# FFT convolution before two gated MLPs on one core: first batch's result kept on chip, exchange laid out slots-innermost, start of the MLP reordered

## The chip, the cores and the metric

The kernel runs on one core of one Trainium2 chip, as one launch. The time is device microseconds for the whole launch. Before the change the median of three runs was 1239.99 us (1238.87 to 1240.51).

## The reference

Two batches of 3008 tokens with 256 channels are convolved along the sequence with a filter given in the frequency domain; the 6016 tokens then pass through a gated MLP (SiLU, hidden width 1536) and a second MLP (a clipped gate, hidden width 2048), all in float32.

```python
X = np.fft.rfft(x, axis=1)                              # x: (2, 3008, 256)
y = np.fft.irfft(X * (filt_r + 1j * filt_i), n=3008, axis=1)
x = y.reshape(6016, 256)
g = x @ w_gate                                          # (256, 1536)
x = (g / (1 + np.exp(-g)) * (x @ w_val)) @ w_out        # w_out: (1536, 256)
h = x @ w_in                                            # (256, 2048)
return (h * np.clip(h + 3, 0, 6) / 6) @ w_out2          # (2048, 256)
```

## The kernel before, in words

**The convolution.** 3008 = 47 x 64, and the transform is split into 64-point and 47-point transforms, each a matrix multiplication on TensorE. For batch 0 there are three steps.

1. `time_to_slots` takes a *unit* of x (128 x 512, `x0_unit(u)`, 12 units), multiplies it by `mat[:, 0]` (float32, two passes), has ScalarE copy the result from PSUM into a staging tile (`stage_tile`, six places in the tags `wq`, `sm`, `y`, `g`) and SyncE (SP) store it to the DRAM tensor `d1[0]`. The 64-point transform gives 32 *slots* (frequencies modulo 64), each with 4 rows (real and imaginary, two halves of the other index).
2. `chunk_view` reads `d1` back the other way round: a *chunk* is one or two slots (17 chunks, `CHUNKS`), with 96 partitions that hold the 4 rows x 24 of the other index. In the loop at L484 a chunk gets a 47-point transform (L488), the filter product on VectorE (`filter_product`, L191 to L194, with the final add on GpSimd, or on VectorE for the last two chunks), the inverse 47-point transform two chunks later (L510), a copy by ScalarE (L200) and a store to `d2[0]` (L201, `store_chunk`). Chunks and filters are loaded six ahead (`load_chunk`, `load_filter`). A filter needs `prepare_filter` first (a ScalarE copy, L179, and a product with a sign, L184 on GpSimd or L182 on ScalarE).
3. `load_near` brings the first 8 time columns back with 128 partitions of slots (`near`, three pieces of 64, 48 and 16 partitions), `to_time` (L216) makes two blocks of 512 tokens out of them, and `split_time` splits them into two fp32r parts (ScalarE L148, VectorE L141): `xsd[0]`, `xsd[1]`. The later blocks read `d2[0]` with `load_g`.

**Batch 1** has its units transformed by the same `time_to_slots` (`staged(u)`, L476): four of them right after the chunk loop, eight in the first step of the MLP loop (`p == 0`, L664 to L666). Its chunks are convolved much later, inside the MLP loop (`conv_...`).

**The MLP.** A loop over `t` (two per *step* `p`) does the first MLP: `gate` and `val` for 128 hidden columns, 12 fp32r matmuls of 512 columns, then SiLU (ScalarE, L656), a product (VectorE, L671), a split of the hidden tile (`plain`: ScalarE L148, VectorE L141), and 12 matmuls of the output layer of the step before. The first 12 steps alternate between `xsd[0]` and `xsd[1]`.

**The weights** arrive as 64-bit floats. `Decode` loads them as pairs of words; `start` (ScalarE, L239) takes an absolute value; `word` is six VectorE instructions (L248 to L255 and an add, which is on GpSimd unless an engine is named); `parts_gv` and `parts_o1` split the result into two fp32r parts for the gate and value columns (512 words) and the output columns (256 words) of one group of 128 hidden units. Groups 0 and 1 are loaded during the chunk loop; `lead` (the 512 words) is decoded at `i == n_chunk`, ahead of the last two chunks' copies, `rest` (the 256) after `xsd[1]`. Groups 2, 3, ... follow in the MLP loop, one per step.

**What sets the order.** The schedule is manual: each engine runs its instructions in the order in which the code issues them. All loads and stores go through SP's queue, except six of the first x units, which ScalarE's queue issues (L413). A store that waits for an engine holds up every DMA behind it. Tiles of one tag share a place, so a new one waits for the old one's readers.

Of the kernel before, what the change touches and what calls it, by code (L numbers as in the profile page):

```python
# [16 lines left out]
P = 128  # L17
# [33 lines left out]
def _matrices():  # L51

    n2 = np.arange(N2)
    s1 = np.zeros((2, N2, NS, 2, 2))
    for h in range(2):
        for s in range(NS):
            if s == 0:
                col = np.ones(N2) if h == 0 else (-1.0) ** n2
            elif h == 0:
                col = np.cos(2 * np.pi * (n2 * s % N2) / N2)  # L60
            else:
                col = -np.sin(2 * np.pi * (n2 * s % N2) / N2)
            for c in range(2):
                s1[c, :, s, c, h] = col
# [23 lines left out]
    t = np.zeros((NS, 2, 2, 2, N2))  # L88
    for s in range(NS):
        for c in range(2):  # L90
            if s == 0:
                t[s, c, 0, c] = 1.0 / S
                t[s, c, 1, c] = (-1.0) ** n2 / S
            else:
                a = 2 * np.pi * (n2 * s % N2) / N2
                t[s, c, 0, c] = 2 * np.cos(a) / S
                t[s, c, 1, c] = -2 * np.sin(a) / S

    m2, m20 = (m.reshape(2, 2, H1, 128).transpose(1, 0, 2, 3) for m in (m2, m20))
    i2, i20 = (m.reshape(128, 2, 2, H1).transpose(0, 2, 1, 3) for m in (i2, i20))  # L100
# [8 lines left out]
def fft_conv_glu_mlp(ctx: ExitStack, tc: tile.TileContext, x, filt, mats, sgn, w1, w2, out):  # L109
# [22 lines left out]
    d1 = [dram.tile([P, H1, D], F32, name=f"d1_{b}") for b in range(B)]  # L132
    d2 = [dram.tile([P, H1, D], F32, name=f"d2_{b}") for b in range(B)]
# [23 lines left out]
    def time_to_slots(b, u, src, stage, tag, pieces=1):  # L157
# [4 lines left out]
        for r in range(pieces):  # L162
            part = slice(r * P // pieces, (r + 1) * P // pieces)
            nc.sync.dma_start(out=d1[b][part, 2 * u:2 * u + 2], in_=stage[part].rearrange("p (m c) -> p m c", c=D))
# [5 lines left out]
    def chunk_view(d, i):  # L170

        s0, n = CHUNKS[i]
        return d.rearrange("(s q h) m c -> (q h m) s c", q=2, h=2)[:, s0:s0 + n]
# [24 lines left out]
    def store_chunk(b, i, acc, q):  # L198
        n = CHUNKS[i][1]
        nc.scalar.copy(out=q[:96, :n].rearrange("p s c -> p (s c)"), in_=acc[:96, :n * D])  # L200
        nc.sync.dma_start(out=chunk_view(d2[b], i), in_=q[:96, :n, :])  # L201

    def load_g(b, j, pool=work):
        g = pool.tile([P, 4, D], F32, tag="g", name="g", bufs=1)
        nc.sync.dma_start(out=g, in_=d2[b][:, 4 * j:4 * j + 4])
        return g
# [51 lines left out]
    def decode_w1(f):  # L258
        return Decode(None, w1[:, f, :], 768, w1_place(f))
# [4 lines left out]
    def parts_o1(d, f, engine):  # L264
        o = [wo1[:, f // 2, h, 0:4:3, :] if f % 2 == 0 else wo1[:, f // 2, h, 1:3, :] for h in range(2)]
        split(o[0], o[1], d.w[:, 512:].rearrange("p (a c) -> p a c", c=P), engine)
# [130 lines left out]
    with tc.manual_schedule():  # L397
# [6 lines left out]
        more0 = early.tile([P, 8192], F32, name="more0")  # L404
        raws = mlp.tile([P, 3584], U32, tag="hs", name="raws", bufs=1)
# [6 lines left out]
        for u in range(12):  # L412
            (nc.scalar if u % 2 else nc.sync).dma_start(out=x0_unit(u), in_=x[0, :, u * 512:(u + 1) * 512])  # L413
# [5 lines left out]
        spare = []  # L419

        def stage_tile():

            if not spare:
                y, g = new_y(), work.tile([P, 1024], F32, tag="g", name="g", bufs=1)
                spare.extend([work.tile([P, 512], F32, tag="wq", name="wq", bufs=1),
                              work.tile([P, 512], F32, tag="sm", name="sm", bufs=1),
                              y[:, :512], y[:, 512:], g[:, :512], g[:, 512:]])
# [4 lines left out]
        def load_chunk(i):  # L432
            s0, n = CHUNKS[i]
            bts[i] = more0[:96, i % 6 * 512:][:, :n * D]
            nc.sync.dma_start(out=bts[i].rearrange("p (s c) -> p s c", c=D), in_=chunk_view(d1[0], i))

        def load_filter(i):
            s0, n = CHUNKS[i]
            fts[i] = x0[:, i % 6 * 1024:][:, :n * 2 * D].rearrange("p (s r c) -> p s r c", r=2, c=D)
            nc.sync.dma_start(out=fts[i][0:N1P], in_=filt[0:N1P, s0:s0 + n])  # L440

        for u in range(12):
            time_to_slots(0, u, x0_unit(u), stage_tile(), "gv" if u % 2 else "a", 4 if u == 11 else 1)
            if u == 7:
                load_filter(0)
        for u in range(6):
            nc.tensor.matmul(bank("gv"), mat[:, 0, :], x0_unit(10 + u % 2))
        for i in range(6):
            load_chunk(i)
            if i:  # L450
# [6 lines left out]
        def w1_place(f):  # L457

            if f < 2:
                raw = raws[:, f * 1536:(f + 1) * 1536]  # L460
                a = more0[:, 3072 + f * 1536:][:, :1536]
            else:
                raw = x0[:, f % 2 * 3072:][:, :1536].bitcast(U32)
                a = x0[:, f % 2 * 3072 + 1536:][:, :1536]
            return raw.rearrange("p (n t) -> p n t", t=2), a[:, :768], a[:, 768:]

        units = list(range(12))

        def x1_unit(u):
            k = u + 12 if u < 4 else u - 4 if u < 10 else u + 2  # L470
            return more0[:, k * 512:(k + 1) * 512]
# [4 lines left out]
        def staged(u):  # L476
            time_to_slots(1, u, x1_unit(u), stage_tile(), "a")
# [5 lines left out]
        lead = slice(0, 512)  # L483
        for i in range(n_chunk + 2):  # L484
            if i < n_chunk:
                acc = bank()
                v = bts.pop(i)
                nc.tensor.matmul(acc[:, :v.shape[1]], mat[:96, 1 + alone(i), :], v)  # L488
# [4 lines left out]
                if i + 6 < n_chunk:  # L493
                    load_chunk(i + 6)
                    load_filter(i + 6)
                if i in (6, 9):
                    dec[len(dec)] = decode_w1(len(dec))
                if i > n_chunk - 5:
                    load_x1(i - (n_chunk - 4))
# [7 lines left out]
            if q >= 0:  # L507
                y = ys.pop(q)
                acc = bank("a")
                nc.tensor.matmul(acc[:96, :y.shape[1]], mat[:, 3 + alone(q), :96], y)  # L510
# [23 lines left out]
        left = units[4:]  # L534
        gt = {}
        dec[2].start()
# [4 lines left out]
        def conv_load(c):  # L541
            if 0 <= c < n_chunk:
                s0, n = CHUNKS[c]
                bt = pool.tile([96, 2, D], F32, tag="bt", name="bt", bufs=2)
                nc.sync.dma_start(out=bt[:, :n, :], in_=chunk_view(d1[1], c))
# [57 lines left out]
        for t in range(2 * n_pair):  # L603
# [60 lines left out]
            if p == 0:  # L664
                for u in left[4 * i:4 * (i + 1)]:
                    staged(u)  # L666
# [25 lines left out]
            if t == 0:  # L692
                dec[3].start()

# [187 lines left out]
```

## Time and profile before

| what | value |
|---|---|
| median of three runs | 1239.99 us (1238.87 to 1240.51) |
| profiled execution, its own time | 1241.09 us |
| its span | 1239.3 us |
| mean granted TensorE clock | 0.987 of full |
| busy: TensorE / VectorE / ScalarE / GpSimd | 97% / 86% / 52% / 16% |
| DMA traffic | 86.08 MB, 69 GB/s over the span |

The 1.8 us between span and time lie outside the program. The busy shares are means over stages with very different limits: the convolution of batch 0 and the start of the MLP fill the first 130 us, and of those alone the change touches the program (the layout of `d1` and `d2` also reaches batch 1's convolution from 199 us on).

### The profile page before, as it was taken

How to read it: one execution, taken by the hardware profiler on the slowest of the kernel's cores; microseconds unless marked ns; L12 is line 12 of the kernel's file. 1: busy time of each engine (PE TensorE's matmuls, PEld its weight loads, DVE VectorE, ACT ScalarE, POOL GpSimd, SP SyncE). 2: the span in 40 equal slices, each digit the busy share in tenths (PEclk: the TensorE clock that was granted, in tenths of full speed). 3: DMA queues.
4: the chain of work that ended last, by engine and by line, in shares of the span. 5: the costliest groups of instructions: out<-in, count | busy, mean ns of one | idle time of the engine just before them, and what ended most of it. 6: DMA issues, size and time to landing. Idle time of an engine off the chain costs nothing.

```text
span 1239.3 us, 17614 instructions
## 1 busy us (share of the span) xinstructions
PE 1197.2 (97%) x6722; PEld 1023.6 (83%) x6722; DVE 1068.7 (86%) x1628; ACT 639.4 (52%) x987; POOL 194.8 (16%) x154
## 2 busy tenths in 40 slices
PE   7869999899999999999999999999999999999997
PEld 3236788788889988888888989999989999899997
DVE  1757766999996888877888899999999999999998
ACT  3635445455554444434444555555655565565554
POOL 1704451431110222201222320000000000000000
PEclk9889999899999999999999999999999999999999
DMA  9975313233312222121120320110011001001000
GB/s 278 256 244 176 102 55 99 65 94 94 94 47 78 82 79 76 44 79 49 52 68 1 110 76 1 35 35 15 21 33 35 19 15 35 34 1 35 33 18 16
DMA packets 45428, 86.08 MB, mean 69 GB/s; under 512 B 4784, under 2 KB 23088, under 8 KB 45216
## 3 DMA queue, kind: packets, MB, share of 16 engines
q1 hardware_dynamic: 44480, 83.39, 22.0%
q10 hardware_dynamic: 864, 1.57, 0.4%
q8 instruction: 53, 0.87, 0.3%
q14 instruction: 31, 0.25, 0.1%
HBM read 56.37 MB, written 28.57 MB: 69 GB/s over the span
## 4 chain that ended last, share of the span: by engine, by line
PE 50%; DVE 43%; issue 3%; DMA 2%; POOL 1%; ACT 1%; SPq 0%; DVEq 0%; ACTq 0%; POOLq 0%
PE gv L153 30%; DVE hs L141 14%; PE a L299 12%; DVE h L821 9%; DVE h L141 8%; DVE h L144 3%; PE a L153 2%; PE gv L216 1%; DVE y L371 1%; DVE y L141 1%; DVE xs L141 1%; PE a L160 1%; DMA x<-filt_in 1%; PE a L510 1%; DVE bs L141 1%
## 5 line engine op out<-in xcount | busy, mean ns | idle before, releaser
L299 PEld LDWEIGHTS a<-hs,wall 128*128 128x128 f32 x3276 | 409.0, 189 | 14.0 <-ACT hs L348 1.1
L153 PE MATMUL gv<-xs,wall 128*128 128x512 f32 (+1 forms) x1728 | 412.6, 392 | 7.9 <-DVE u L194 4.4
L299 PE MATMUL a<-hs,wall 128*128 128x256 f32 (+1 forms) x3276 | 416.7, 282 | 2.2 <-ACT hs L348 0.9
L141 DVE TENSOR_TENSOR hs<-h,hs 128x768 fp32r<-128x768 f32 (+2 forms) x324 | 361.9, 1117 | 30.0 <-ACT hs L148 16.6
L153 PEld LDWEIGHTS gv<-xs,wall 128*128 128x128 f32 x1728 | 321.0, 189 | 75.2 <-DVE u L194 5.6
L153 PE MATMUL gv<-xs,wi 128*128 128x512 f32 (+1 forms) x1152 | 275.9, 388 | 0.0
L341 ACT CAST hs<-h 128x768 fp32r<-128x768 f32 (+1 forms) x156 | 128.2, 821 | 261.6 <-DVE h L821 159.7
L153 PEld LDWEIGHTS gv<-xs,wi 128*128 128x128 f32 x1152 | 210.0, 188 | 37.0 <-DVE xs L141 0.4
L348 ACT CAST hs<-h 128x1024 fp32r<-128x1024 f32 (+1 forms) x156 | 160.7, 1030 | 67.4 <-DVE h L141 67.4
L141 DVE TENSOR_TENSOR h<-h 128x512 f32<-128x512 f32 (+3 forms) x312 | 182.4, 585 | 8.7
L671 DVE TENSOR_TENSOR h<-h,gv 128x512 f32<-128x512 f32 (+1 forms) x144 | 96.4, 670 | 40.7 <-PE gv L153 38.4
L821 DVE SCALAR_TENSOR_TENSOR h<-h,gv 128x512 f32<-128x512 f32 (+1 forms) x192 | 128.5, 669 | 0.0
L656 ACT ACTIVATE h<-gv 128x512 f32<-128x512 f32 (+1 forms) x144 | 84.5, 587 | 62.9 <-PE gv L153 62.4
L817 ACT ACTIVATE h<-gv 128x512 f32<-128x512 f32 (+1 forms) x192 | 111.8, 582 | 0.9 <-PE gv L153 0.9
L144 DVE TENSOR_TENSOR h<-h 128x256 f32<-128x256 f32 (+1 forms) x156 | 68.1, 436 | 5.4
L144 POOL TENSOR_TENSOR ww<-ww,wa 128x512 f32<-128x512 f32 x16 | 20.7, 1295 | 216.3 <-DVE wa L255 216.3
L144 POOL TENSOR_TENSOR u<-u,t 128x512 f32<-128x512 f32 (+1 forms) x17 | 20.8, 1225 | 146.0 <-DVE u L194 90.9
L153 PE MATMUL a<-hs,wall 128*128 128x512 f32 x144 | 35.8, 397 | 3.2 <-DVE hs L141 3.2
L191 DVE SCALAR_TENSOR_TENSOR us<-gv,x 64x512 f32<-64x512 f32 (+1 forms) x17 | 11.2, 662 | 32.0 <-PE gv L488 23.4
L153 PEld LDWEIGHTS a<-hs,wall 128*128 128x128 f32 x144 | 26.8, 188 | 10.5 <-DVE hs L141 4.5
L148 ACT CAST hs<-h 128x1024 fp32r<-128x1024 f32 x12 | 12.7, 1058 | 36.9 <-DVE h L671 31.6
L148 ACT CAST xs<-gv 128x512 fp32r<-128x512 f32 (+1 forms) x20 | 11.5, 576 | 37.3 <-PE gv L216 37.3
(110 smaller groups left out, 822.6 us busy)
## 6 DMA issues: line engine op xcount, KB each, us to landing
raw<-w_in SPq DMA_DIRECT2D x16, 512.0 KB, 4.5
x<-w_in SPq DMA_DIRECT2D x10, 768.0 KB, 4.3
g<-d SPq DMA_DIRECT2D x10, 512.0 KB, 3.9
yd<-y SPq DMA_DIRECT2D x10, 512.0 KB, 2.9
g<-yd SPq DMA_DIRECT2D x10, 512.0 KB, 3.7
y_out<-y SPq DMA_DIRECT2D x20, 256.0 KB, 2.3
ft<-filt_in SPq DMA_DIRECT2D x15, 256.0 KB, 3.5
wt<-wd SPq DMA_DIRECT2D x8, 448.0 KB, 3.2
```

The costliest lines, as they stand in the source:

```text
L141: (engine or nc.vector).tensor_tensor(out=out, in0=a, in1=b, op=ALU.subtract)
L144: (engine or nc.vector).tensor_tensor(out=out, in0=a, in1=b, op=ALU.add)
L148: nc.scalar.copy(out=hi, in_=src)
L153: nc.tensor.matmul(acc, w, v, start=first and i == 0, stop=last and i == 2)
L160: nc.tensor.matmul(acc, mat[:, 0, :], src)
L299: nc.tensor.matmul(acc[b][:, 256 * h:256 * h + nt], w[:, r, iw], hs[:, v, ih, :nt], start=first and h == 0 and v == 0 and r == 1, stop=las ...
L341: nc.scalar.copy(out=self.parts(0, 0, 3), in_=v(1, 4))
L348: nc.scalar.copy(out=self.parts(0, 3, 7), in_=self.values(4, 8))
L656: nc.scalar.activation(out=h, in_=hid[p].halves(gate), func=AF.Silu)
L671: nc.vector.tensor_tensor(out=h, in0=h, in1=hid[p].halves(val), op=ALU.mult)
L817: nc.scalar.activation(out=h, in_=pre, func=AF.Relu, bias=3.0)
L821: nc.vector.scalar_tensor_tensor(out=h, in0=h, scalar=6.0, in1=pre, op0=ALU.min, op1=ALU.mult)
```

## The change

- `d1` and `d2` are laid out `[24, 128, 256]` instead of `[128, 24, 256]`, and the 128 rows go (4 rows, 32 slots) with slots innermost. A chunk's two slots are now one run of 2 KB per partition instead of two of 1 KB; a stored unit becomes two runs of 1 KB per partition instead of one of 2 KB, and `near` and `g` are read in runs of 1 KB.
- The result of batch 0's chunks is copied into one tile, `qall` (96 x 32 slots x 256). Of each chunk 32 of 96 partitions, those that `near` needs, are stored at once; the other 64 are stored later in two transfers of 1 MB.
- `near` is loaded in two rounds of four: 24 partitions each once 15 chunks are stored, and 8 each at the end.
- Buffers for four chunks and filters ahead instead of six, with filters 0 and 1 loaded in the first stage.
- Groups 0 and 1 load only their 512 words of gate and value in the chunk loop; both are decoded after the last chunk's copy. Their 2 x 256 words of the output layer come in one later load, `both`, decoded as one.
- Of batch 1's units three are transformed ahead of the MLP (was four) and nine in steps 1 to 9, one each (was eight in step 0).
- All x loads are issued by SP; extra matmuls without use (`idle`) stand before the first unit and around the first chunks.

```diff
+    def rows(d, s0, n):
+        return d.rearrange("m (g s) c -> (m g) s c", g=4)[:, s0:s0 + n]
-    d1 = [dram.tile([P, H1, D], F32, name=f"d1_{b}") for b in range(B)]
-    d2 = [dram.tile([P, H1, D], F32, name=f"d2_{b}") for b in range(B)]
+    d1 = [dram.tile([H1, P, D], F32, name=f"d1_{b}") for b in range(B)]
+    d2 = [dram.tile([H1, P, D], F32, name=f"d2_{b}") for b in range(B)]
...
+        nc.sync.dma_start(out=d1[b].rearrange("m p c -> p m c")[:, 2 * u:2 * u + 2],
+                          in_=stage.rearrange("p (m c) -> p m c", c=D))
...
+        a = x0[:, f % 2 * 3072:][:, :3072]
+        return Decode(None, w1[:, f, :], 768, (words(a[:, :1536]), a[:, 1536:2304], a[:, 2304:]))
...
-            (nc.scalar if u % 2 else nc.sync).dma_start(out=x0_unit(u), in_=x[0, :, u * 512:(u + 1) * 512])
+            nc.sync.dma_start(out=x0_unit(u), in_=x[0, :, u * 512:(u + 1) * 512])
...
+        idle(8, P)
...
-            if u == 7:
-                load_filter(0)
-        for u in range(6):
-            nc.tensor.matmul(bank("gv"), mat[:, 0, :], x0_unit(10 + u % 2))
-        for i in range(6):
+            if u in (7, 9):
+                load_filter(u // 2 - 3)
+        idle(8, 384)
+        for i in range(4):
             load_chunk(i)
...
         def load_near(a, b):
-            nc.sync.dma_start(out=near[a:b], in_=d2[0][a:b, :8])
+            for r in range(a, P, NS):
+                nc.sync.dma_start(out=near[r:r + b - a], in_=d2[0].rearrange("m p c -> p m c")[r:r + b - a, :8])
...
+                if i < 4:
+                    idle(1, 384)
...
-                if i + 6 < n_chunk:
-                    load_chunk(i + 6)
-                    load_filter(i + 6)
+                if i + 4 < n_chunk:
+                    load_chunk(i + 4)
+                    load_filter(i + 4)
...
-            if i == n_chunk:
-                for f in range(2):
-                    dec[f].word(nc.vector, lead)
-                    parts_gv(dec[f], f, nc.vector)
...
-                store_chunk(0, q, acc, stage_tile().rearrange("p (s c) -> p s c", c=D))
-            if q == 10:
-                load_near(0, 64)
+                nc.scalar.copy(out=qall[:96, s0 * D:(s0 + n) * D], in_=acc[:96, :n * D])
+                nc.sync.dma_start(out=rows(d2[0], s0, n)[0:32], in_=qs[0:32, s0:s0 + n])
+            if q == 14:
+                load_near(0, 24)
...
-        load_near(64, 112)
-        load_near(112, 128)
-        for u in units[:4]:
+        load_near(24, 32)
+        for f in range(2):
+            d = dec.pop(f)
+            d.word(nc.vector)
+            parts_gv(d, f, nc.vector)
+        for u in range(3):
             staged(u)
...
-        for u in units[4:]:
-            load_x1(u)
         dec[2] = decode_w1(2)
         dec[3] = decode_w1(3)
+        for a in range(0, NS, 16):
+            nc.sync.dma_start(out=rows(d2[0], a, 16)[32:96], in_=qs[32:96, a:a + 16])
...
-        rest = slice(512, 768)
+        a = side[:, :2048]
+        both = Decode(None, w1[:, 0:2, 1024:], 512, (words(a[:, :1024]), a[:, 1024:1536], a[:, 1536:]))
+        both.start()
+        both.word(nc.vector)
         for f in range(2):
-            d = dec.pop(f)
-            d.word(nc.vector, rest)
-            parts_o1(d, f, nc.vector)
+            parts_o1(both, f, nc.vector, both.w[:, f * 256:(f + 1) * 256])
...
-            if p == 0:
-                for u in left[4 * i:4 * (i + 1)]:
-                    staged(u)
+            if 1 <= p < 10 and i == 1:
+                staged(p + 2, "gv")
...
+            if p < 9 and i == 0:
+                load_x1(p + 3)
```

The order of the instructions at the three places that matter, each engine's own list. First SP's queue from the last chunks' stores to the first weights of the MLP loop; before (`d_0_74` is batch 0's `d2`, `d_1_73` batch 1's `d1`, `more_103` and `raws` hold x units and raw weights):

```order
L201 DMA d_0_74<-sm 96x2x256
L474 DMA more_103<-x_in 128x512
L201 DMA d_0_74<-y 96x2x256 x2
L201 DMA d_0_74<-g 96x256
L480 DMA near<-d_0_74 48x2048
L480 DMA near<-d_0_74 16x2048
L164 DMA d_1_73<-g 128x512
L164 DMA d_1_73<-wq 128x512
L164 DMA d_1_73<-sm 128x512
L164 DMA d_1_73<-y 128x512
L474 DMA more_103<-x_in 128x512 x8
L234 DMA x_102<-w_in 128x1536 x2
```

And now:

```order
L517 DMA d_0_74<-qall 32x512 x2
L484 DMA near<-d_0_74 24x8x256 x4
L517 DMA d_0_74<-qall 32x512
L517 DMA d_0_74<-qall 32x256
L484 DMA near<-d_0_74 8x8x256 x4
L162 DMA d_1_73<-wq 128x2x256
L162 DMA d_1_73<-sm 128x2x256
L162 DMA d_1_73<-y 128x2x256
L232 DMA x_102<-w_in 128x1536 x2
L536 DMA d_0_74<-qall 64x4096 x2
L232 DMA side<-w_in 128x2x512
```

The near loads went from two pieces here to eight, the eight x loads left, and behind the weights of groups 2 and 3 stand the two deferred stores and then the load `both` (`side<-w_in`).

Second, ScalarE from the last chunks' copies to the first SiLU; before:

```order
L200 COPY y<-a 96x512
L148 CAST wall<-more_103 128x512 x2
L200 COPY y<-a 96x512
L200 COPY g<-a 96x256
L161 COPY g<-a 128x512
L161 COPY wq<-a 128x512
L161 COPY sm<-a 128x512
L161 COPY y<-a 128x512
L148 CAST xs<-a 128x512 x4
L148 CAST wall<-more_103 128x2x128
L148 CAST wall<-more_103 128x256
L239 ACTIVATE x_102<-x_102 128x768
```

And now:

```order
L516 COPY qall<-a 96x512 x2
L516 COPY qall<-a 96x256
L148 CAST wall<-y 128x512
L148 CAST wall<-g 128x512
L161 COPY wq<-a 128x512
L161 COPY sm<-a 128x512
L161 COPY y<-a 128x512
L148 CAST xs<-a 128x512 x4
L237 ACTIVATE side<-side 128x512
L148 CAST wall<-side 128x2x128
L148 CAST wall<-side 128x256
L237 ACTIVATE x_102<-x_102 128x768
```

The last two chunk copies moved ahead of the casts of the decoded weights (`wall`), and the start of `both` (`side<-side`) stands new between the splits of `xsd` and the start of group 2.

Third, TensorE from the first blocks on; before:

```order
L216 MATMUL a<-mat,near 128x128 x16
L153 MATMUL gv<-xs,wall 128x512 x12
L160 MATMUL a<-more_103,mat 128x512 x4
L153 MATMUL gv<-xs,wall 128x512 x12
L160 MATMUL a<-more_103,mat 128x512 x4
L153 MATMUL gv<-xs,wall 128x512 x24
L153 MATMUL a<-hs,wall 128x512 x12
```

And now:

```order
L214 MATMUL a<-mat,near 128x128 x16
L153 MATMUL gv<-xs,wall 128x512 x48
L153 MATMUL a<-hs,wall 128x512 x12
L160 MATMUL gv<-qall,mat 128x512
L153 MATMUL gv<-xs,wall 128x512 x24
L153 MATMUL a<-hs,wall 128x512 x12
L160 MATMUL gv<-qall,mat 128x512
```

The eight unit transforms left step 0; one now stands behind each of nine output-layer groups.

## Rows read from the trace of the kernel before

**Rows 1.** The page's slices of the span (40 of 31 us), busy tenths.

```profile
DMA  9975313233312222121120320110011001001000
```

**Rows 2.** Windows: us; busy us (count) of PE, PEld, DVE, ACT, POOL; PEclk, DMA share, GB/s.

```profile
24.00:30.00 6.00, 2.90 (x5) 0.74 (x4) 3.73 (x7) 1.23 (x2) 2.75 (x3) 0.67 1.06 208
66.00:68.00 2.00, 1.28 (x4) 0.24 (x2) 1.91 (x6) 1.27 (x3) 0.00 (x0) 1.00 0.95 211
69.00:72.00 3.00, 1.86 (x3) 0.88 (x4) 2.25 (x4) 0.62 (x1) 0.00 (x0) 0.74 1.07 397
84.00:93.00 9.00, 9.00 (x47) 7.74 (x46) 4.53 (x10) 2.25 (x4) 0.00 (x0) 0.81 1.04 384
130.00:199.00 69.00, 69.00 (x308) 56.35 (x308) 46.90 (x59) 29.95 (x50) 29.66 (x22) 1.00 0.23 69
```

**Rows 3.** The chain that ended last, in order of time: start, us, what.

```profile
67.00 0.43 DVE us L144
...
70.17 0.70 DVE more L144
...
77.23 2.00 DMA d<-g
79.24 4.11 DMA near<-d
...
96.69 0.11 ACT x L239
...
111.80 0.81 ACT x L239
...
121.57 0.82 ACT x L239
...
129.71 3.06 PE a L153 x12
132.77 5.57 PE gv L153 x24
```

**Rows 4.** Timeline of VectorE: the first instruction of a chunk's filter product.

```profile
25.73 0.69 DVE L191 SCALAR_TENSOR_TENSOR us<-gv,x 64x512 f32<-64x512 f32 x1 [0.97 <-POOL x L184]
...
36.42 0.69 DVE L191 SCALAR_TENSOR_TENSOR us<-gv,x 64x512 f32<-64x512 f32 x1 [1.57 <-ACT sm L200]
...
55.64 0.69 DVE L191 SCALAR_TENSOR_TENSOR us<-gv,x 64x512 f32<-64x512 f32 x1
60.67 0.69 DVE L191 SCALAR_TENSOR_TENSOR us<-gv,x 64x512 f32<-64x512 f32 x1 [2.92 <-ACT g L200]
```

**Rows 5.** Timeline of ScalarE: filters as they land, then the end of the chunk loop.

```profile
30.05 0.62 ACT L179 COPY x<-x 64x512 f32<-64x512 f32 x1 [1.54 <-DMA x<-filt_in]
36.31 0.62 ACT L179 COPY x<-x 64x512 f32<-64x512 f32 x1 [0.87 <-DMA x<-filt_in]
...
66.70 0.57 ACT L200 COPY y<-a 96x512 f32<-96x512 f32 x1
75.71 0.62 ACT L148 CAST wall<-more 128x512 fp32r<-128x512 f32 x1 [4.20 <-DVE more L144]
78.62 0.58 ACT L161 COPY sm<-a 128x512 f32<-128x512 f32 x1 [0.58 <-PE a L160]
```

**Rows 6.** DMA issues of the first 100 us: queue, KB each, median us to landing.

```profile
x<-filt_in SPq DMA_DIRECT2D x15, 192.0 KB, 7.1
near<-d SPq DMA_DIRECT2D x1, 384.0 KB, 5.0
d<-g SPq DMA_DIRECT2D x4, 64.0 KB, 1.7
near<-d SPq DMA_DIRECT2D x1, 128.0 KB, 4.1
```

**Rows 7.** The chain again, one unit transform of the first stage.

```profile
16.90 0.86 PE gv L160 x2
```

**Rows 8.** Waits of TensorE from 88 to 131 us: us in total, times, longest.

```profile
PE a L153 <- DVE hs L141: 3.2, 3, 1.3
```

More of the change, by code (lines that the diff above doesn't have):

```diff
@@ L53, in _matrices @@
     n2 = np.arange(N2)
-    s1 = np.zeros((2, N2, NS, 2, 2))
+    s1 = np.zeros((2, N2, 2, 2, NS))
     for h in range(2):
@@ L91, in _matrices @@
             if s == 0:
-                t[s, c, 0, c] = 1.0 / S
-                t[s, c, 1, c] = (-1.0) ** n2 / S
+                t[c, 0, s, c] = 1.0 / S
+                t[c, 1, s, c] = (-1.0) ** n2 / S
             else:
                 a = 2 * np.pi * (n2 * s % N2) / N2
[L96 to L100, printed above, removed]
+                t[c, 0, s, c] = 2 * np.cos(a) / S
+                t[c, 1, s, c] = -2 * np.sin(a) / S
+    m2, m20 = (m.reshape(2, 2, H1, 128).transpose(2, 1, 0, 3) for m in (m2, m20))
+    i2, i20 = (m.reshape(128, 2, 2, H1).transpose(0, 3, 2, 1) for m in (i2, i20))
     mats = np.zeros((P, 6, P), np.float32)
@@ L153, in products3, with time_to_slots @@
             nc.tensor.matmul(acc, w, v, start=first and i == 0, stop=last and i == 2)
-    def time_to_slots(b, u, src, stage, tag, pieces=1):
+    def time_to_slots(b, u, src, stage, tag):
         acc = bank(tag)
@@ L198, in store_chunk @@
     def store_chunk(b, i, acc, q):
-        n = CHUNKS[i][1]
+        s0, n = CHUNKS[i]
         nc.scalar.copy(out=q[:96, :n].rearrange("p s c -> p (s c)"), in_=acc[:96, :n * D])
-        nc.sync.dma_start(out=chunk_view(d2[b], i), in_=q[:96, :n, :])
+        nc.sync.dma_start(out=rows(d2[b], s0, n), in_=q[:96, :n, :])
     def load_g(b, j, pool=work):
         g = pool.tile([P, 4, D], F32, tag="g", name="g", bufs=1)
-        nc.sync.dma_start(out=g, in_=d2[b][:, 4 * j:4 * j + 4])
+        nc.sync.dma_start(out=g, in_=d2[b].rearrange("m p c -> p m c")[:, 4 * j:4 * j + 4])
         return g
@@ L403, in fft_conv_glu_mlp @@
         x0 = early.tile([P, 6144], F32, name="x0")
-        more0 = early.tile([P, 8192], F32, name="more0")
-        raws = mlp.tile([P, 3584], U32, tag="hs", name="raws", bufs=1)
+        qall = early.tile([P, 8192], F32, name="qall")
+        qs = qall.rearrange("p (s c) -> p s c", c=D)
+        side = mlp.tile([P, 3584], F32, tag="hs", name="side", bufs=1)
         near = work.tile([P, 8, D], F32, tag="xs", name="near")
@@ L418, in fft_conv_glu_mlp, with idle @@
         nc.sync.dma_start(out=sg, in_=sgn)
-        spare = []
+        def idle(n, cols):
+            acc = bank()
+            for _ in range(n):
+                nc.tensor.matmul(acc[:, :cols], mat[:, 0, :], mat.rearrange("p a c -> p (a c)")[:, :cols])
+        idle(8, P)
+        spare, turns = [], []
         def stage_tile():
             if not spare:
-                y, g = new_y(), work.tile([P, 1024], F32, tag="g", name="g", bufs=1)
                 spare.extend([work.tile([P, 512], F32, tag="wq", name="wq", bufs=1),
-                              work.tile([P, 512], F32, tag="sm", name="sm", bufs=1),
-                              y[:, :512], y[:, 512:], g[:, :512], g[:, 512:]])
+                              work.tile([P, 512], F32, tag="sm", name="sm", bufs=1)])
+                if len(turns) < 3:
+                    y, g = new_y(), work.tile([P, 1024], F32, tag="g", name="g", bufs=1)
+                    spare.extend([y[:, :512], y[:, 512:], g[:, :512], g[:, 512:]])
+                turns.append(len(spare))
             return spare.pop(0)
@@ L544, in conv_load @@
                 bt = pool.tile([96, 2, D], F32, tag="bt", name="bt", bufs=2)
-                nc.sync.dma_start(out=bt[:, :n, :], in_=chunk_view(d1[1], c))
+                nc.sync.dma_start(out=bt[:, :n, :], in_=rows(d1[1], s0, n))
                 ft = pool.tile([P, 2, 2, D], F32, tag="ft", name="ft", bufs=3)
```

64 lines of the change are left out of this document (27 added, 37 removed).

## The prediction

> **What bounds the kernel now.** I read the page's slices first. The DMA engines are full in the first two slices and busy in the third [rows 1]; after 130 us DMA hardly counts, so a change of layouts and transfers can act before that only. The windows say what follows: from 130 to 199 us TensorE is busy 69.00 of 69.00 us at full clock [rows 2]. The order of every engine is fixed, so what arrives early or late at 130 us is handed on to the end, unless TensorE gets more work behind it. I therefore count two things: when the run of matmuls at 129.71 us [rows 3] begins, and what is added after it.
>
> Ahead of it there are two stages. In the chunk loop VectorE starts a chunk every (55.64 - 36.42) / 9 = 2.14 us when nothing is missing [rows 4]. From 25.73 us at this pace the third chunk after it would start at 32.1, not 36.42: 4.3 us lost to filters that land (36.31 - 30.05) / 3 = 2.09 us apart [rows 5]; and 60.67 stands where 57.8 was due: 2.9 us lost, about the second load of weights. The loop's last VectorE instruction ends at 67.43 [rows 3]; call this moment E. In the tail ScalarE's last chunk copies stand behind the casts of the decoded weights (the second cast starts at 75.71, E + 8.3) [rows 5]; the last store issues at 77.23, near lands at 83.35 (E + 15.9), and group 2's decode starts at 96.69 (E + 29.3) [rows 3]. From there a chain of decodes (Abs on ScalarE, word on VectorE, add on GpSimd, cast) leads in 33.0 us to 129.71.
>
> **The change part by part.**
>
> *Chunk loop: E moves from 67.43 to 62.8.* Four chunks are asked for instead of six and filters 0 and 1 come in the first stage, so the 4.3 us go. Filter 1 adds 192 KB there; at 208 to 384 GB/s [rows 2] that is 0.5 to 0.9 us, and I take 0.7. Units stored in runs of 1 KB I cost at nothing: from 69 to 72 us stores in 1 KB runs stood in the queue and 397 GB/s flowed; the other end is the 208 GB/s of the stretch of 1 KB chunk loads [rows 2], which would add 6.9 us for 3.1 MB, but filters share that stretch. The weights of groups 0 and 1 shrink from 768 to 512 KB, so the 2.9 us become 1.9 (bounds 0, if lighter traffic absorbs them, and 4.3, since four buffers give less lead than six). E = 67.4 - 4.3 + 0.7 - 1.0 = 62.8. Storing 32 instead of 96 partitions takes DMA work that VectorE's pace already hides. The idle matmuls stand where TensorE waits for x or for chunks: nothing; without that cover, the eight of 384 columns would cost what the old six of 512 did.
>
> *Tail, near.* The copy of the 15th chunk stays at E - 0.7 [rows 5], so round one of near (four pieces of 24 partitions) issues from E + 0.3 to E + 1.5 and lands 4.4 us after that, between the 4.1 of 16 and the 5.0 of 48 partitions [rows 6]: E + 5.9. The last two stores are behind it in the queue and need 1.7 us of their own: E + 7.6. (They would land at E + 4.1 if the queue didn't hold them; a filter's 7.1 us [rows 6] say it does.) Round two issues over 1.2 us and its last piece, nearest to the one of 16 partitions, takes 4.1: E + 12.9, not E + 15.9. The ends are E + 7.0 and, one piece after the other at 4.1, E + 24.
>
> Here a rule speaks against the change. Loads into 64 partitions ran at 211 GB/s and into 128 at 384 [rows 2]. The Trainium skill (SBUF — State Buffer, "Door 1: The DMA port swizzle") says that a transfer's rate goes by how many of 16 ports its partitions reach, about 27 GB/s each; the rows agree for 64 (8 ports) and 128. By it pieces of 24 partitions reach six ports and of 8 two, each round would take an estimated 4.8 us of transfer, near would land at about E + 14, and the sum would be 1.1 us more than mine.
>
> *Tail, weights of the output layer.* This takes near's place as the last wait. The casts end as before, three unit copies of 0.58 us [rows 5] follow, and SP can issue the units' stores, groups 2 and 3, the two deferred stores and then `both` only from E + 10.6. All of it is 0.8 + 1.6 + 2.1 + 0.5 = 5.0 MB ahead of `both`'s last byte: 13.0 us at 384 GB/s [rows 2]. The nearest rows for the deferred stores' rate are the stretch with stores, 397, and the load into 64 partitions, 211, which would add 4.5 us [rows 2]; I take the store's. Starting when near is through: E + 12.9 + 13.0 = E + 25.9 (ends E + 23.6, if near holds nothing, and E + 30.4). ScalarE and VectorE stand behind it: Abs 0.6 by the copy of 512 columns, word 3.4 (67.43 to 70.87 [rows 3]), two casts of about 0.4, since one of 512 columns takes 0.62 [rows 5]. Group 2 starts at E + 30.7, later against E than before (29.3): what near gains, the shared load takes back. In time: 62.8 + 30.7 = 93.5, against 96.69: **3.2 us earlier**.
>
> *From there to the run of matmuls: 33.0 us, unchanged.* The eight units that leave step 0 (8 x 0.86 us [rows 7]) and their copies lay beside the decode chain, whose order is kept.
>
> *The nine units in steps 1 to 9 are the price.* Each is 0.86 us of TensorE [rows 7]. TensorE waits 3.2 us in that chain for VectorE's splits [rows 8], which take two of them. The other seven fall where it is always busy: 7 x 0.86 = **6.0 us later**. The ends are 0 and nine times 0.86, 7.7. Their x loads and stores are asked for a step ahead, with DMA at 0.23 busy [rows 2]: nothing. If an x load came late, TensorE would stand in front of it.
>
> *Batch 1 and the g loads* get the new runs; 0.23 busy DMA hides them, and nothing in the chain from 130 us waits on them.
>
> The sum: -3.2 + 6.0 = +2.8 us on the profiled execution's 1241.09 us, which stands 1.1 above the median: 1239.99 + 2.8 = **1242.8 us**. Its own range is 1240.5 to 1246.
>
> **The rivals.**
>
> *The near pieces hold nothing, and the weight loads stall nothing (even).* Then `both` lands at E + 23.6, group 2 starts at E + 28.4, and E is 60.9: 89.3, 7.4 earlier, less 6.0: 1238.6. For it: the DMA engines have free stretches in a lighter loop. Against: 64 partitions ran at 211 GB/s [rows 2].
>
> *The units are hidden (faster).* If the decode chain, not TensorE, sets the pace of steps 3 to 9, the units cost nothing: 3.2 earlier, 1236.8. It decides at 8.36 + 0.86 = 9.2 us per step (8.36 is 36 matmuls at 5.57 per 24 [rows 3], the pace of the run): group 4 to group 5 took 121.57 - 111.80 = 9.8 us [rows 3], which speaks for it. Against: 69.00 of 69.00 busy later [rows 2].
>
> *The new row distance slows the chunks (slower still).* Each chunk row now lies 32 KB from the next; before, four rows of one slot lay together. If its 192 KB move at 211 instead of 384 GB/s [rows 2], a chunk costs 0.42 us more, over 16 chunks 6.7: 1249.5. For it: filter rows lie 64 KB apart, and the stretch with them ran at 208 [rows 2]. Against: those go to 48 partitions only. The Trainium skill (DMA: Bandwidth & Descriptors, "Latency and other measured facts") states slower copies for row distances of large powers of two, from 512 KB up; no run here has shown it at 32 KB.
>
> *The change doesn't do what it says.* If round two's pieces go one after the other, near lands at E + 24, later than before, and `both` at E + 37: 1253.9.
>
> **How the numbers follow.** A measurement of this kernel tells about 0.2%, 2.5 us, from no change: the bounds are 1237.5 and 1242.5. Chances: my forecast 0.46, even 0.24, hidden units 0.14, row distance 0.13, near one by one 0.03. Faster: the hidden units and the even case's low side, 0.20. Same: the rest of the even case and the part of the forecast's range under 1242.5, 0.36. Slower: 0.44. The range 1236.5 to 1249.5 reaches from the hidden units to the row distance and leaves out less than 2 in 10.
>
> **What would show it.** Right: VectorE's last chunk instruction near 63 us; near landing about 13 us after it; ScalarE's Abs on the shared load waiting for DMA until about E + 26; group 2's Abs at 93 to 94; the run of matmuls from about 126.5 with 9.2 us per step. Wrong: E at 67 or later (row distance), steps of 9.2 us or more with TensorE waiting (hidden units), or `both` landed well before ScalarE asks for it.

## The result and the profile after

The changed kernel takes **1248.46 us** (median of four runs, 1247.28 to 1250.55), the kernel before 1240.25 (1238.87 to 1241.17): a ratio of **1.0069**, 95% interval 1.0052 to 1.0086. It is slower by 8.2 us where 2.8 were forecast. The profiled execution took 1247.8 us, its span is 6.7 us longer than before.

The page's slices, first, against [rows 1]: the first four read 8, 8, 7, 3 where they read 9, 9, 7, 5. DMA has lost load, and the time did not follow.

```profile
span 1246.0 us, 17673 instructions
DMA  8873423323311222121120320110111001101100
```

VectorE's timeline of the changed kernel (start, us, line, operation; in brackets the idle time before it and what ended it) answers to [rows 4].

```profile
26.44 0.43 DVE L189 SCALAR_TENSOR_TENSOR us<-gv,x 64x256 f32<-64x256 f32 x1 [26.44 <-DMA mat<-mats_in]
29.42 0.69 DVE L189 SCALAR_TENSOR_TENSOR us<-gv,x 64x512 f32<-64x512 f32 x1 [1.67 <-issue]
32.14 0.69 DVE L189 SCALAR_TENSOR_TENSOR us<-gv,x 64x512 f32<-64x512 f32 x1 [0.60 <-POOL us L144]
...
36.83 0.69 DVE L189 SCALAR_TENSOR_TENSOR us<-gv,x 64x512 f32<-64x512 f32 x1 [0.43 <-PE gv L491]
...
66.31 0.42 DVE L144 TENSOR_TENSOR us<-us 128x256 f32<-128x256 f32 x1
```

The first chunk starts at 26.44 (before the change 23.45), the fifth at 36.83, where [rows 4] have 36.42, and the loop's last instruction ends at **E = 66.73**. Forecast was 62.8.

Behind E the timelines of SP, TensorE and ScalarE show the tail, against the near, cast and Abs (absolute value, the first step of a decode) rows of [rows 3, 5]:

```profile
66.35 1.69 SPq L484 DMA_DIRECT2D near<-d  x4
73.73 1.32 SPq L484 DMA_DIRECT2D near<-d  x4
79.85 5.24 PE L214 MATMUL a<-mat,near 128*128 128x128 f32 x32 [9.76 <-DMA d<-wq]
80.17 0.54 SPq L232 DMA_DIRECT2D side<-w_in  x1
93.11 0.66 ACT L237 ACTIVATE side<-side 128x512 f32<-128x512 f32 x1 [6.91 <-DMA side<-w_in]
97.97 0.89 ACT L237 ACTIVATE x<-x 128x768 f32<-128x768 f32 x1
```

Round two of near issues at E + 7.0 (forecast 7.6); the matmuls on near start at E + 13.1 (near was to land at 12.9; its landing is not among the recorded events, and the store named in the third row is none that these matmuls need, so E + 13.1 is only the latest that it can have been); ScalarE waits 6.91 us for the shared weights, which are there at E + 26.4 (25.9); group 2's Abs is at E + 31.2 (30.7). The chain of waits goes the same way and shows the units of batch 1 between the steps:

```profile
80.17 12.91 DMA side<-w_in
...
98.07 0.80 ACT x L237
...
131.61 2.80 PE a L153 x12
134.41 0.86 PE gv L160 x2
135.27 5.59 PE gv L153 x24
140.86 2.80 PE a L153 x12
143.66 0.86 PE gv L160 x2
```

The last of these units runs at 189.66 us, so the change reaches beyond the first 130 us. The span splits into E and what lies behind it: 67.43 + 1171.9 before, 66.73 + 1179.3 after. In these two executions all of the loss is behind E.

### The profile page after: what moved, and what is told of

Its sections match the earlier page's. It is cut to its first block, busy times and chain, and to the rows that moved or that the text cites. A ratio compares the mean times of both kernels' runs of the same rounds, so it can differ in the third digit from the quotient of the medians.

```text
span 1246.0 us, 17673 instructions
## 1 busy us (share of the span) xinstructions
PE 1196.8 (96%) x6750; PEld 1029.3 (83%) x6750; DVE 1068.7 (86%) x1622; ACT 640.4 (51%) x988; POOL 195.6 (16%) x154
## 4 chain that ended last, share of the span: by engine, by line
PE 56%; DVE 36%; DMA 3%; issue 2%; ACT 1%; SPq 0%; POOL 0%; DVEq 0%; ACTq 0%; POOLq 0%
PE gv L153 34%; PE a L299 15%; DVE hs L141 12%; DVE h L833 7%; DVE h L141 7%; PE a L153 3%; DVE h L144 3%; PE gv L214 1%; DVE y L371 1%; DVE y L141 1%; DMA side<-w_in 1%; DVE xs L141 1%; PE gv L160 1%; DMA x<-filt_in 1%; DMA d<-g 1%
## 5 line engine op out<-in xcount | busy, mean ns | idle before, releaser
L144 DVE TENSOR_TENSOR h<-h 128x256 f32<-128x256 f32 (+1 forms) x156 | 68.1, 436 | 5.3
L189 DVE SCALAR_TENSOR_TENSOR us<-gv,x 64x512 f32<-64x512 f32 (+1 forms) x17 | 11.2, 662 | 31.3 <-DMA mat<-mats_in 26.4
L153 PEld LDWEIGHTS a<-hs,wall 128*128 128x128 f32 x144 | 28.0, 196 | 10.4 <-DVE hs L141 3.9
L144 POOL TENSOR_TENSOR x<-x 128x768 f32<-128x768 f32 x10 | 20.1, 2009 | 67.6 <-issue 39.8
```

The costliest lines, as they stand in the source:

```text
L144: (engine or nc.vector).tensor_tensor(out=out, in0=a, in1=b, op=ALU.add)
L153: nc.tensor.matmul(acc, w, v, start=first and i == 0, stop=last and i == 2)
```

## The experiments

Each kernel was timed beside the kernel before on its own chip, so the ratios compare. "Behind E" is the profiled span less E; its rows come from one execution each.

| kernel | median us | ratio (95% interval) | E | behind E |
|---|---|---|---|---|
| before | 1240.25 | 1 | 67.43 | 1171.9 |
| changed | 1248.46 | 1.0069 (1.0052 to 1.0086) | 66.73 | 1179.3 |
| e1_units_p0 | 1242.43 | 1.0021 (1.0006 to 1.0036) | 68.70 | 1172.2 |
| e2_both_first | 1243.22 | 1.0021 (1.0010 to 1.0032) | 68.06 | 1173.7 |
| e3_pieces | 1249.72 | 1.0069 (1.0041 to 1.0096) | 68.68 | 1179.0 |
| e4_casts_last | 1233.81 | 0.9941 (0.9918 to 0.9964) | 64.78 | 1167.2 |
| e5_d1_old | 1248.62 | 1.0079 (1.0063 to 1.0095) | 68.04 | 1179.1 |
| e6_six | 1246.62 | 1.0075 (1.0045 to 1.0104) | 69.89 | 1181.1 |
| e7_no_idle | 1248.03 | 1.0074 (1.0055 to 1.0092) | 69.40 | 1177.5 |
| e8_three | 1238.97 | 1.0006 (0.9995 to 1.0016) | 66.55 | 1172.0 |
| e9_six_d1_old | 1246.06 | 1.0052 (1.0032 to 1.0071) | 66.83 | 1178.1 |
| e10_near_one | 1233.79 | 0.9954 (0.9937 to 0.9971) | 70.05 | 1164.2 |
| e11_four_filters | 1249.87 | 1.0087 (1.0069 to 1.0105) | 70.59 | 1179.4 |
| e12_weights_late | 1245.07 | 1.0055 (1.0039 to 1.0070) | 64.80 | 1178.2 |

### The units in steps 1 to 9

```diff
-            if 1 <= p < 10 and i == 1:
-                staged(p + 2, "gv")
+            if p == 0:
+                for u in range(3 + 4 * i, 7 + 5 * i):
+                    staged(u)
```

Their loads move with them, behind the shared weights.

> The changed kernel with its nine remaining units of batch 1 taken out of steps 1 to 9 and put back beside the decode chain of step 0 (their x loads all behind the shared weight load). If the units cost TensorE time in its full stretch (7 x 0.86 us), the time falls by 6.0 us, from 1248.5 to 1242.5, with the run of matmuls starting where it did (131.6). Rival, the decode chain sets the pace and hides them: within 1 us of 1248.5. Second rival, the nine x loads and stores beside the decode chain disturb it: the run of matmuls starts 1 to 3 us later and half of the gain is gone.

Measured: 1242.43. The run of matmuls starts at 131.92 and, in the chain, its blocks follow each other with no unit between:

```profile
131.92 3.06 PE a L153 x12
134.98 5.60 PE gv L153 x24
140.58 2.80 PE a L153 x12
143.38 5.60 PE gv L153 x24
```

A step is 8.40 us here (143.38 - 134.98) and 9.25 in the changed kernel (143.66 - 134.41). Behind E 7.1 us are gone: 5.4 after the start of the run, against 6.0 expected, and 1.7 ahead of it (E + 63.2 in place of 64.9), which was not expected. In the run a unit costs what TensorE needs for it; the rival that a decode chain hides them has fallen.

### The shared weight load

```diff
         del a, d
+        a = side[:, :2048]
+        both = Decode(None, w1[:, 0:2, 1024:], 512, ...)
         for u in range(3):
             staged(u)
```

> The changed kernel with the load of the shared output weights asked for right behind the words of groups 0 and 1, ahead of the three units' stores, groups 2 and 3 and the deferred stores. If this load is the last wait of the tail (landed 26.4 us behind E), it now lands some 15 to 18 us behind E, the second half of near (E + 13.1) with its splits is the last wait, and group 2's Abs starts about 8 us earlier (E + 23): 1240.5. Rival, the queue gives back what it gains (near and groups 2 and 3 come later by as much, or another wait stands right behind): within 1.5 us of 1248.5.

Measured: 1243.22, and 5.6 us less behind E: the cause holds, the expected size was 8. Near's matmuls and ScalarE show why:

```profile
81.31 6.66 PE L214 MATMUL a<-mat,near 128*128 128x128 f32 x32 [9.88 <-DMA side<-w_in]
88.00 1.08 ACT L148 CAST xs<-a 128x512 fp32r<-128x512 f32 x2 [2.32 <-DMA x<-w_in]
88.97 0.68 ACT L237 ACTIVATE side<-side 128x512 f32<-128x512 f32 x1
94.00 0.89 ACT L237 ACTIVATE x<-x 128x768 f32<-128x768 f32 x1
```

The matmuls on near start at E + 13.2, nearly where the changed kernel has them, ScalarE no longer waits for the shared load, but its Abs, word and casts still stand behind near's splits: 94.00 is E + 25.9, not E + 23. (The DMAs named in the first two rows are only the last events that the profile saw; the casts of the second row need near's matmuls, which end at 87.97.)

### Both large parts and the old first exchange together

e8 is e1, e2 and the edit of e5 (below) in one kernel.

> The changed kernel with three things together: the nine units beside the decode chain (alone 6.0 us faster), the shared weight load first (alone 5.2 us faster), and d1 in the old layout with the last unit in pieces. If the three add up, 1248.5 - 6.0 - 5.2 - 2.0 = 1235.3, within 2 us of the kernel before with only the casts moved (1233.8). Rival, the nine x loads and stores beside the decode chain now meet the weight loads of groups 2 and 3, which are the last wait there: the two large gains add up to 8 rather than 11, and the time is 1238.

Measured: 1238.97 on a chip where the kernel before took 1238.03. By the ratios (1.0006 against 1.0069) that is 7.8 us faster than the changed kernel, near the 8 of the rival. The chain shows a collision, and it is one of places rather than of rates:

```profile
79.58 10.66 DMA d<-qall
90.26 3.43 DMA qall<-x_in
93.82 6.34 PE a L160 x8
```

The nine x loads go into `qall`, whose deferred rows are stored until 90.24; only then may they issue, and TensorE's units in step 0 wait for them until 93.82. e1 alone already has this wait:

```profile
90.25 4.42 DMA qall<-x_in
```

Against E both begin the run of matmuls at the same place (E + 63.3 and E + 63.2), and behind E they take the same (1172.0 and 1172.2): there the shared load first brought nothing on top of e1. Other places for x were not tried.

### The order of the tail alone

The kernel before, with the words and casts of groups 0 and 1 behind the last stores and near, and nothing else:

```diff
-            if i == n_chunk:
-                for f in range(2):
-                    dec[f].word(nc.vector, lead)
-                    parts_gv(dec[f], f, nc.vector)
...
         load_near(112, 128)
+        for f in range(2):
+            dec[f].word(nc.vector, lead)
+            parts_gv(dec[f], f, nc.vector)
```

> The kernel before the change, with one thing done alone: the words and casts of groups 0 and 1 moved from the loop's end behind the last stores and near's loads, as the change has it. If ScalarE's casts ahead of the last two chunk copies are what held near (last store at E + 9.8, near landed at E + 15.9), the last store issues at about E + 2, near lands at E + 8, group 2's Abs starts about E + 22 in place of E + 29.3, and the time falls by some 7 us, to 1233. Rival, the casts themselves are then what is late (they stand on ScalarE ahead of the units and the splits in any case): at most 1 to 2 us faster, 1238.5 to 1240.

Measured: **1233.81, ratio 0.9941**. Timelines of ScalarE, SP and TensorE:

```profile
68.11 0.37 ACT L200 COPY g<-a 96x256 f32<-96x256 f32 x1 [2.50 <-issue]
68.50 0.32 SPq L201 DMA_DIRECT2D d<-g  x1
77.17 5.44 PE L216 MATMUL a<-mat,near 128*128 128x128 f32 x32 [4.12 <-DMA near<-d]
90.28 0.89 ACT L239 ACTIVATE x<-x 128x768 f32<-128x768 f32 x1
```

and from its chain near's landing:

```profile
72.19 4.74 DMA near<-d
```

The last store issues at E + 3.7 (before E + 9.8), near lands at 76.93, E + 12.2 (E + 15.9), group 2's Abs at E + 25.5 (E + 29.3). Behind E 4.7 us are gone, in one execution; the rest of the gain is in that execution's E. So a part of the change that pays is the order of three lines; the units in the steps and the place of the shared weight load give it back: without either the changed kernel is 5 to 6 us faster (e1, e2), without both 7 to 8 (e8).

Near in one load, after all stores, on top of it:

```diff
-            if q == 10:
-                load_near(0, 64)
...
-        load_near(64, 112)
-        load_near(112, 128)
+        load_near(0, 128)
```

> The kernel before the change with the casts of groups 0 and 1 behind the last copies (alone 6.4 us faster) and with near asked for in one load of 128 partitions behind all stores, in place of 64 partitions in the middle of them and the rest behind. In the run with the casts moved alone, SP stood at the first of near's loads until 61.65 with four stores and four x loads behind it, ScalarE's last copy waited 2.5 us for a store's place, and near landed at 76.9. If this load in the queue is what is late, the last store issues near 66 instead of 68.5, near lands at about 74.5, and the time falls by another 2 us, to 1231.5. Rival, the words and casts of groups 0 and 1, whose second cast ends at 73.8, and the units behind them leave no room: within 0.7 us of 1233.5. Second rival, one load of 1 MB from 24 KB rows takes longer than the second half alone did (4.7 us): 1 to 2 us slower.

Measured: 1233.79. Behind E another 3.0 us went, but the intervals of e4 and e10 overlap and no gain in time is shown. In e10's chain VectorE's words of groups 0 and 1 hold the tail, not near:

```profile
77.61 0.70 DVE more L144
...
78.86 0.59 ACT g L161
...
79.49 5.62 PE a L216 x32
```

### What holds E

Two edits of the first stage. e3 stores the last unit in four pieces again; e5 does so too and puts d1 back into the old layout (slots outermost).

```diff
+        for r in range(pieces):
+            part = slice(r * P // pieces, (r + 1) * P // pieces)
```

> The changed kernel with the last unit of the first stage stored in four pieces of 32 partitions (64 KB each) again, as before the change. If the landing of this one 256 KB store (3.67 us, where pieces of 64 KB took 1.7) is the main part of the first stage's lost 2.9 us, the first chunk load issues 2 us earlier (about 21.2 in place of 23.18), E moves from 66.7 to about 65, and the time is 1246.5. Rival, the filters set the ramp (filter 2 landed at 30.18): the first chunk comes earlier, E does not move, 1248.5. Second rival, the 1 KB runs of all stores hold the queue: the first chunk load does not move either.

> The changed kernel with d1, the exchange after the first product, in the old layout (slots outermost, 2 KB runs) and with the last unit's store in four pieces again; d2 stays new. In the old layout a chunk's rows are neighbouring slots, so the first chunk needs only the first of the four pieces; in the new one each chunk takes slots from all four quarters of a unit's store, and the first chunk load waits for all of the last unit. If that is the first stage's loss, the first chunk load issues at about 21 (new layout, four profiles: 22.3 to 23.4), E is 2 us earlier, and the time is 1246.5. Rival, the filters' pace of 2.1 us each sets E whatever the first chunk does (as when the pieces alone were put back): 1248.5. Second rival, the 1 KB runs cost as well: ScalarE's waits for the stores (2.8 us) go too, E is 3 us earlier or more, 1245 or less.

Measured: 1249.72 and 1248.62. SP's timeline of e3, then of e5:

```profile
18.98 2.52 SPq L164 DMA_DIRECT2D d<-g  x5
23.40 0.78 SPq L450 DMA_DIRECT2D x<-d  x2
```

```profile
18.00 2.33 SPq L164 DMA_DIRECT2D d<-g  x5
21.92 0.78 SPq L454 DMA_DIRECT2D x<-d  x2
```

Pieces alone move nothing: with slots innermost a chunk takes rows from all four quarters of a unit. With the old layout, where the first chunk needs the first piece alone, it issues 1.5 us earlier, but 1.0 of that is there before the last stores are asked for (18.00 in place of 18.98). The stretch that compares is the one from the end of ScalarE's last unit copy to the first chunk load. Before, then in the changed kernel:

```profile
17.80 0.58 ACT L161 COPY g<-gv 128x512 f32<-128x512 f32 x1 [0.23 <-PE gv L160]
20.32 0.78 SPq L435 DMA_DIRECT2D more<-d  x2
```

```profile
18.42 0.59 ACT L161 COPY g<-gv 128x512 f32<-128x512 f32 x1
23.18 0.79 SPq L448 DMA_DIRECT2D x<-d  x2
```

That stretch is 1.9 to 2.0 us with the loop before the change (before, e4, e10), 4.0 to 4.2 with the new layout (changed, e1, e2, and e3 with its pieces) and 3.4 to 3.6 with d1's old layout and pieces (e5, e8, e9). By these the layout accounts for 0.5 to 0.8 us of the 2.1 lost; what holds the rest no run separates. ScalarE's waits for stores, which the second rival of e5 wanted gone, are still there (3.2 us). The time is the changed kernel's in both, so the first stage is not shown to be what E waits for, and d1's row distance costs nothing that the time shows.

Four edits of the loop: six places in place of four (e6), the same with d1's old layout (e9), no idle matmuls (e7), filters 2 and 3 in the first stage (e11).

> The changed kernel with six places for chunks and filters in place of four (the chunks in columns of the weights' tile that are written much later), asked for six ahead, as before the change. If four places are what leaves VectorE waiting (1.1 us at the fifth chunk, 2.9 to 4.7 about the second load of weights), E is 2 to 3 us earlier and the time 1246. Rival, depth only queues the same transfers: the stalls move into the ramp (filters landing one after the other, as before the change, 8.2 us of waits in all), within 1 us of 1248.5.

> The changed kernel with six places for chunks and filters and with d1 in the old layout, last unit in pieces: both runs before this one together. With six places and the new layout the filters landed 2.35 us apart through the whole loop (29.74 to 48.74 in eight steps), with the DMA engines at 1.05 of their time: the transfers, not VectorE's 2.14 us, set the pace. With four places the depth hides which. If the new layout of d1 is what slows the transfers, the filters now land 2.1 us apart as before the change (30.05 to 38.36 in four steps), VectorE's last chunk ends near 66 and not at 69.9, and the time is 1244 to 1246. Rival, d1's layout has no part in it (the rest of the change has): 2.35 us again, VectorE's last chunk near 68 to 69 and the time within 1.5 us of the changed kernel, 1248.

> The changed kernel without the four pairs of idle matmuls in the first four chunks of the loop (no part of the result). They run 1.28 us at half clock ahead of the second chunk's product, for which VectorE waits 1.1 to 1.7 us. If they cost time, the second chunk starts 1.3 us earlier and the time falls by 1 to 1.5 us, to 1247. Rival, filter 2, which lands at 30, takes it back at the third chunk: 1248.5, no change. Second rival, without them the granted clock falls later in the loop and it is 1 us slower.

> The changed kernel with filters 2 and 3 also asked for in the first stage (behind units 8 and 10), so that all four places are filled before the first chunk load. In three profiles with the changed kernel's loop VectorE's fifth chunk starts 10.4 to 10.9 us behind its first, where its own pace gives 8.6, and the waits stand where filters 2 and 3 land. If filters that come late are what holds the ramp, the fifth chunk now starts 8.6 to 9.2 us behind the first; the first comes 0.7 to 1.4 us later for the 384 KB; E is about 1 us earlier and the time 1247.5. Rival, the same bytes have to pass in any case and the wait only moves (to the chunk loads, or to filters 4 and 5): the ramp shortens by as much as the first stage grows, E and the time stay within 0.7 us of 1248.5. Second rival, the ramp is set by GpSimd's and TensorE's chain behind each chunk: it stays at 10.5 us and the time is 1 us longer.

Measured: 1246.62, 1246.06, 1248.03 and 1249.87; each interval overlaps the changed kernel's. Windows from 36 to 48 us (busy of PE, PEld, DVE, ACT, POOL; clock, DMA share, GB/s) of e6, then e9:

```profile
36.00:48.00 12.00, 9.60 (x22) 3.29 (x20) 10.14 (x15) 7.86 (x16) 8.60 (x8) 1.00 1.06 180
```

```profile
36.00:48.00 12.00, 8.96 (x20) 3.09 (x19) 11.28 (x17) 7.68 (x15) 9.45 (x9) 1.00 1.08 194
```

With six places the engines of the DMA are hardly free (shares of 1.06 and 1.08), the filters land 2.38 us apart in e6 (29.74 to 48.74 in eight steps; the 2.35 above is a slip) and 2.28 in e9, and VectorE's chunks follow at their pace. d1's old layout does not bring back the 2.1 us. E came 3.1 us earlier in e9 than in e6 (66.83 and 69.89), as the main expectation had it, but one loop's executions differ by nearly as much and the times' intervals overlap: whether d1's layout has a small part in it stays open. In e11 the fifth chunk starts 9.6 us behind the first (10.4 in the changed kernel), but the first starts at 28.07: the wait has moved, as the rival said, and grown. Without idle matmuls (e7) the ramp, from the first chunk to the fifth, takes 12.2 us, and the time is the same. Windows from 30 to 36 us of the kernel before, the changed one and e7 (clock third from the end):

```profile
30.00:36.00 6.00, 6.00 (x8) 2.18 (x8) 3.21 (x5) 3.59 (x7) 5.16 (x5) 0.50 1.10 187
```

```profile
30.00:36.00 6.00, 5.97 (x14) 2.68 (x14) 5.23 (x9) 3.23 (x7) 5.37 (x6) 0.86 0.85 181
```

```profile
30.00:36.00 6.00, 4.41 (x7) 1.80 (x7) 3.53 (x6) 2.90 (x6) 5.20 (x5) 0.50 0.94 172
```

The weights of groups 0 and 1, asked for at chunks 12 and 13:

```diff
-                if i in (6, 9):
+                if i in (12, 13):
```

> The changed kernel with the two 512 KB loads of groups 0 and 1 asked for at chunks 12 and 13, behind the last filter, in place of chunks 6 and 9. Profiles with the changed kernel's loop show VectorE waiting 1.8 to 4.7 us in the chunks behind the second of these loads. If the loads push the filters back, this wait goes, E is 2 to 3 us earlier, the weights land by E - 2 in time for ScalarE's Abs, and the time is 1246. Rival, the wait is not theirs, or the Abs then waits for them at the loop's end: within 0.7 us of 1248.5.

Measured: 1245.07; the interval overlaps the changed kernel's, so the gain in time is not established. In the trace the wait is gone. VectorE in e12, then in the changed kernel:

```profile
51.51 0.69 DVE L189 SCALAR_TENSOR_TENSOR us<-gv,x 64x512 f32<-64x512 f32 x1
53.77 0.69 DVE L189 SCALAR_TENSOR_TENSOR us<-gv,x 64x512 f32<-64x512 f32 x1 [0.15 <-PE gv L491]
64.38 0.42 DVE L144 TENSOR_TENSOR us<-us 128x256 f32<-128x256 f32 x1
```

```profile
52.28 0.69 DVE L189 SCALAR_TENSOR_TENSOR us<-gv,x 64x512 f32<-64x512 f32 x1 [0.55 <-POOL x L182]
55.69 0.69 DVE L189 SCALAR_TENSOR_TENSOR us<-gv,x 64x512 f32<-64x512 f32 x1 [1.30 <-PE gv L491]
```

E is 64.80, the lowest of the kernels with the changed loop. The chunks about the two loads of 512 KB cost VectorE waits of 1.9 us in the changed kernel, and 3.3 to 4.7 in e1, e2 and e3.

## Why the prediction held behind E and failed ahead of it

The sign was right; the size was short by 5.4 us, and nearly all of that is one term. That the time lies inside the stated range is luck: it is beyond the forecast's own range (1240.5 to 1246), and the upper end, 1249.5, comes from the row distance, which did not bring it about.

**Behind E: right.** The forecast was 1.4 us for the tail (E + 30.7 in place of 29.3) and 6.0 for the units, 7.4 in all. The profile has 7.4: 2.0 to group 2's Abs, 0.6 from there to the run of matmuls (33.6 in place of 33.0) and 4.8 after it. The shared load did take near's place as the last wait, and e2 shows that by moving it alone. That the sum meets to 0.1 us is in part luck: two terms were 0.6 short and the units 1.2 too high. Near's round two issued 0.6 us early and was through at most 6.1 us later; the forecast had 5.3 from the rows. By the ports of the Trainium skill (SBUF — State Buffer, "Door 1: The DMA port swizzle") the same sum came to an estimated 6.4, and the trace does not decide between the two. The row of 211 GB/s that the prediction read as loads into 64 partitions is no pure one either: SP issued two x units and two stores in those two us.

**Ahead of E: the step that failed is "E moves from 67.43 to 62.8".** Three profiles each have the loop of one side: 67.4, 64.8, 70.1 with that of before (before, e4, and e10, which lacks near's first load in it), 66.7, 68.7, 68.1 with the changed one (changed, e1, e2). The means are 67.4 and 67.8 (66.1 before without e10): no gain in E shows. By its parts, each a mean of three:

- *First stage*, +0.7 forecast: the first chunk starts at 25.6 in place of 24.1, +1.6. ScalarE's last unit copy ends no later (18.6 in place of 19.0); what was left out is the 2.1 us more from there to the first chunk load. With slots innermost it waits for all of the last unit's store, which by e5, e8 and e9 is 0.5 to 0.8 of them; the rest is open.
- *The ramp*, -4.3 forecast: from the first chunk to the fifth 10.7 us in place of 12.4, -1.7. I put the whole loss down to filters that land one after the other. Two of the four places are filled early now, and the third filter still lands at 30.18, 7.0 us behind the first chunk load's issue, as the chunks, the matrices and the filter share the DMA engines ahead of it. The ramp goes with the granted clock from 30 to 36 us: 11.7 to 13.0 us at 0.50 to 0.66 (before, e4, e10), 10.4 to 10.9 at 0.86 to 1.00 (changed, e1, e2), and in e7, with the filters early and no idle matmuls, 12.2 at 0.50, the lower of the two clock levels (1.2 GHz). In that execution the early filters brought next to nothing, so the 1.7 us seem to come from the idle matmuls, which I had put at nothing; one execution does not show it.
- *The loop from the fifth chunk on*, -1.0 forecast: 31.5 us in place of 31.0, +0.5. Lighter loads of the weights did not shorten the stall; in e12's trace, with the loads behind the last filter, it is gone.

Together they were to move E by -4.6 and moved it by +0.4. With +0.4 in place of -4.6 the forecast's own sum is 7.8; measured are 8.2.

**The rivals.** "Near holds nothing" and "the units are hidden" fell with the profile and e1. "The new row distance" gave nearly the right time (1249.5) for the wrong reason: e5 has the old distance in d1 and the same time. The Trainium skill (DMA: Bandwidth & Descriptors, "Latency and other measured facts") speaks of row distances from 512 KB on; no run here shows a cost of d1's 32 KB in time. "Round two one by one" fell: near was there by E + 13.1.

**Open.** Why the changed loop, with two thirds of its stores taken out, moves no faster than the loop before isn't settled: d1's layout, depth, idle matmuls and early filters were each undone or changed (d1's layout with the last unit in pieces) without E coming earlier than in the kernel before, the place of the weights explains some 3 us in one execution, and d2's layout and the x loads all on one queue were not tried alone.

## What to carry to other kernels

Split the span at a moment that both kernels have, and sum ahead of it and behind it apart: queue orders and counted matmuls behind it came out to 0.1 us in the sum and 0.6 to 1.2 in the terms, a stage that shares the DMA engines missed by 5. When a layout is turned, ask which stores each load now has to wait for, not only how long the runs are. When a change has several parts, run the cheapest alone: three lines moved gave -0.59%, the whole change, which has them in it, +0.69%.

## What had not been expected of the hardware

The loop of the kernel before ended at 64.8 and 67.4 us in two executions, the changed one at 66.7, 68.1 and 68.7. A spread of 2 to 3 us is about half of the gain that I had forecast for it; one profile of such a stage is no measure of it. And a DMA share of 1 is no sign of a full rate: from 36 to 48 us the changed kernel moved 228 GB/s at a share of 0.78, the same kinds of transfers asked for six deep (e6) 180 at 1.06.

```profile
DMA packets 1243, 2.73 MB, mean 228 GB/s; under 512 B 255, under 2 KB 287, under 8 KB 1241
q1 hardware_dynamic: 1241, 2.71, 78.2%
```

That is 121 ns for a packet (0.782 x 16 x 12 us / 1241) in the changed kernel; in e6 the same line has 1036 packets at 105.4%, 195 ns each, of nearly the same size (2.2 and 2.1 KB). That depth alone does it is not shown: the kernel before asked six deep as well and moved 242 GB/s at 1.10 in the same window, with 2155 packets of 1.3 KB and 98 ns each.
